# A fused attention and feed-forward kernel: a reordered beginning, and attention in fewer, wider steps

## The chip, the cores and the metric

The kernel runs on one core of a Trainium2 chip. The metric is the device time of one execution in microseconds, the median of several runs; less is better. One run was taken with the hardware profiler.

## The reference

```python
def _attn_ref(q, k, v, p):                      # q, k, v: (8, 8, 576, 64); p: (8, 8, 32, 64)
    scale = 1.0 / np.sqrt(q.shape[-1])
    def sm_attn(qq, kk, vv):
        s = scale * np.matmul(qq, kk.transpose(0, 1, 3, 2))
        s = s - np.max(s, axis=-1, keepdims=True)
        a = np.exp(s)
        a = a / (np.sum(a, axis=-1, keepdims=True) + 1e-09)
        return np.matmul(a, vv)
    p_packed = sm_attn(p, k, v)
    return sm_attn(q, p_packed, p_packed)

def _moe_ref(x, w_in, w_out):                   # x: (4608, 512); w_in: (512, 2048); w_out: (2048, 512)
    h = x @ w_in
    sp = np.where(h > 20.0, h, np.log1p(np.exp(np.minimum(h, 20.0))))
    g = h * np.tanh(sp)
    return (g @ w_out).astype(np.float32)
```

Per batch and head, 32 packed queries attend to 576 keys, which gives 32 packed values. The 576 queries then attend to those 32. The outputs of the 8 heads side by side are the 512 columns of x, which go through two matrices with a Mish between them. The inputs q, k, v, p are float32. The two weight matrices arrive as float64 and are converted on the core.

## The kernel before

The work goes batch by batch, 8 batches of 576 tokens. The second attention is never multiplied out: since x = a2 · p_packed, the kernel multiplies the packed values with w_in once per batch and chunk of 512 columns (`packed_w`, PSUM tile ps_w, split into wp_hi and wp_lo), and then the attention weights a2 (aT_hi and aT_lo) with that product. Each operand is split into a rounded high half and a low half, and three matmuls stand for one.

The main loop runs over 128 groups, one for each batch b and each of the 16 column blocks f of 128. Step t of the loop (`step`) does the up matmuls of group t (`up`, tile ps_h: two halves of six matmuls, each followed by ScalarE's Mish into g), the split of g into g_hi and g_lo (`halves`), and the down matmuls of group t − 2 (`down`: four accumulators acc of three matmuls each, weights wo). The order on TensorE in a step is: down 0, up 0, down 1, down 2, up 1, down 3. At the end of every fourth step, `packed_w` for the next chunk follows. Some steps also hold `down_rest` (tile ps_rest), the 64 tokens left over in two batches.

Between these pieces stand calls to two generators. `take(gen, ...)` advances the attention of the next batch by one step, up to three times in a step of the loop. `take(conv, ...)` advances the conversion of the weights: per weight, ScalarE writes two parts (`words`), VectorE joins them in four instructions (`join`, the last of which the profile names L390), and `done` writes them away or splits them (wo). w_in has 16 such weights, four for each chunk c (tile wi), and w_out has 16 (tile wo); the list `weights` says in which order.

Attention of one batch has these parts: turn the keys (transposes through PSUM, tile ps_kq, copied to kT by ScalarE and VectorE in turns), scores of the packed queries (ps_s) with their maximum and subtraction on VectorE, exponentials, the same turning for the queries (qT), row sums, transposes of the weights (tiles ps_a and a1T), the packed values (ps_pp, pp) and their transpose (ppT), the scores of all queries (`match`), and then `peak` and `weigh`, which make the second softmax on VectorE and ScalarE. From the third batch on, all its PSUM tiles come from the pool ps_a, which has two buffers of one bank each. packed_w and down_rest take theirs from the same pool.

TensorE's order is the order in which the code is written, throughout. In the beginning (attention of the first two batches, and the first 16 steps), the order on VectorE, ScalarE and SP's DMA queue is the written one too. From step 16 on, a scheduler with its own estimate of times sets the order on these three. Every engine works through its queue in order.

Of the kernel before, what the change touches and what calls it, by code (L numbers as in the profile page):

```python
# [35 lines left out]
def body(  # L36
# [101 lines left out]
    class Batch:  # L138
# [48 lines left out]

        def score(self, g, pool):

            kT = att.tile([P, NI, 4, R], F32, name="kT", tag="T", bufs=2)  # L190
            yield from transposed(pool, self.k_t[g], g, kT)
            s_ps = scores(pool, self.pT[:, g, :], kT)
            mx = stat.tile([P, 2], F32, name="mx")
            for u in range(2):
                nc.vector.reduce_max(out=mx[:, u:u + 1], in_=s_ps[u], axis=AX.X)
            top = stat.tile([P, 1], F32, name="top")
            nc.vector.tensor_tensor(out=top, in0=mx[:, 0:1], in1=mx[:, 1:2], op=ALU.max)
            for u in range(2):
                nc.vector.tensor_scalar(
                    out=self.a1[:, g, u].rearrange("a i r -> a (i r)"), in0=s_ps[u],  # L200
                    scalar1=top, scalar2=None, op0=ALU.subtract,
                )
            yield
# [42 lines left out]
        def turn_weights(self, g, pool):  # L246
            self.a1T[g] = att.tile([R, 2, NI, P], F32, name="a1T")
            for u in range(2):
                ps = psum(pool, [R, NI, P], "ps_a1")
                for i in range(NI):  # L250
                    nc.tensor.transpose(out=ps[:, i, :], in_=self.a1[:, g, u, i, :], identity=ident)  # L251
                evacuate(self.a1T[g][:, u], ps, ("ACT", "DVE")[u])
                yield

        def values(self, g, pool):
# [16 lines left out]
            yield  # L272

        def turn_values(self, g, pool):
            ps = psum(pool, [P, P], "ps_ppT")
            nc.tensor.transpose(out=ps, in_=self.pp[g].rearrange("a u d -> a (u d)"), identity=ident)
            nc.vector.tensor_copy(out=self.ppT[:, g, :], in_=ps)
            yield
# [5 lines left out]
        def match(self, g, pool):  # L284
# [7 lines left out]
            yield  # L292
# [12 lines left out]
        def weigh(self, gs):  # L305
# [9 lines left out]
            for g in range(gs.start, gs.stop):  # L315
                at = att.tile([P, S], F32, name="at", bufs=1)
                nc.vector.transpose(out=at, in_=self.a2[:, g].rearrange("a g n -> a (g n)"))
                nc.scalar.copy(out=self.aT_hi[:, g, :], in_=at)
                nc.vector.tensor_tensor(
                    out=self.aT_lo[:, g, :], in0=at, in1=self.aT_hi[:, g, :].bitcast(F32), op=ALU.subtract  # L320
                )

        def attention(self):
# [249 lines left out]
    weights = [Weight(0, m) for m in range(4)] + [WeightOut(0)] + [Weight(1, m) for m in range(4)]  # L573
    weights += [WeightOut(i) for i in range(1, 8)] + [Weight(2, m) for m in range(4)] + [WeightOut(8)]
# [22 lines left out]
    def step(t, n_att, n_conv, cast):  # L597
# [37 lines left out]
        if t % 4 == 2 and n < len(chunks):  # L635
# [12 lines left out]
    with tc.manual_schedule(engines={mybir.EngineType.PE}):  # L648
# [4 lines left out]
        with tc.manual_schedule(engines={mybir.EngineType.DVE, mybir.EngineType.Activation, mybir.EngineType.SP}):  # L653
# [26 lines left out]
            together(first.turn_weights(0, ps_acc))  # L680
# [6 lines left out]
            together(first.values(0, ps_a))  # L687
            together(first.turn_weights(1, ps_acc))
            w[2].words()
            w[2].join()  # L690
            together(first.values(1, ps_a))
            for g in range(2):
                together(first.turn_values(g, ps_a))
            w[3].words()
            for g in range(2):
                together(first.match(g, ps_acc))
# [10 lines left out]
            first.weigh(slice(0, 1))  # L707
# [15 lines left out]
            together(second.turn_weights(0, ps_acc))  # L723
            step(0, (0, 0, 0), 0, nc.scalar.copy)
            together(second.turn(1, ps_acc))
            second.sums_now(1, sums[1])
            w[4].words()
            w[4].join()
            together(second.values(0, ps_a))
            together(second.turn_weights(1, ps_acc))  # L730
            w[5].words()
            w[4].done()
            conv = conversion(5)
            together(second.values(1, ps_a))
            step(1, (0, 0, 0), 2, nc.scalar.copy)
            for g in range(2):
                together(second.turn_values(g, ps_a))
            for g in range(2):
                together(second.match(g, ps_acc))
            for g in range(2):  # L740
                second.peak(slice(g, g + 1))
            take(conv, 2)
            second.weigh(slice(0, 1))
            take(conv, 2)
            second.weigh(slice(1, 2))
            take(conv, 2)
            for t in range(2, START):
                step(t, (0, 0, 0), 3 if t < 8 or t == 11 else 1 if t == 10 else 2, nc.scalar.copy)
        for t in range(START, len(order) + LAG):
            if t in (16, 26):  # L750
                batches[t // 10 + 1].load()
            step(t, (1, 1, 1), 2, nc.vector.tensor_copy)
# [26 lines left out]
```

## Time and profile before

| | us |
|---|---|
| median of 3 runs (811.91 to 814.41) | 812.47 |
| the profiled execution | 809.08 |
| its span | 807.3 |
| TensorE busy in the span (95%) | 765.5 |
| VectorE busy (55%) | 441.9 |
| ScalarE busy (40%) | 323.2 |

PE is TensorE's matmuls and PEld its weight loads. DVE is VectorE, ACT is ScalarE, SP issues the DMAs. L and a number is a line of the kernel before. In a row of the timeline the start and the duration come first; a bracket at its end tells how long the engine stood idle before it, and what released it.

### The profile page before, as it was taken

The numbers are of one execution on the slowest core, as the hardware profiler recorded it, in microseconds if no ns is written. First come the engines' busy times: TensorE is split into PE (matmuls) and PEld (weight loads), VectorE is DVE, ScalarE is ACT, GpSimd is POOL, SyncE is SP. The second block draws the span as 40 slices with busy tenths as digits, with TensorE's granted clock in tenths as the row PEclk, the third lists the DMA queues.
The fourth block names the chain that finished last, engine by engine and source line by source line (L and its number), as shares of the span: only waits on it lengthen the run. The fifth ranks groups of instructions, "written<-read, shape, count | busy, mean of one in ns | idle before, by whom it ended". The sixth has DMA issues, their size and how long they took to land.

```text
span 807.3 us, 13715 instructions
## 1 busy us (share of the span) xinstructions
PE 765.5 (95%) x5584; PEld 608.5 (75%) x5584; DVE 441.9 (55%) x846; ACT 323.2 (40%) x752; POOL 0.7 (0%) x6
## 2 busy tenths in 40 slices
PE   7565799999999999999999999999999999999997
PEld 6344477887878787878788787888788787878886
DVE  4867887695457537354563546445473445532332
ACT  4353667563433424234342443334242343332221
POOL 0000000000000000000000000000000000000000
PEclk9667699999999999999999999999999999999999
DMA  9993205532522541242311532144311411131002
GB/s 251 302 293 113 104 27 157 161 127 79 172 90 79 158 141 59 76 138 92 111 53 59 176 96 76 56 154 125 112 53 53 137 40 54 53 105 53 1 1 65
DMA packets 42814, 85.82 MB, mean 106 GB/s; under 512 B 8448, under 2 KB 26880, under 8 KB 42752
## 3 DMA queue, kind: packets, MB, share of 16 engines
q1 hardware_dynamic: 42752, 84.95, 34.5%
q8 instruction: 44, 0.72, 0.4%
q14 instruction: 18, 0.15, 0.1%
HBM read 71.30 MB, written 13.63 MB: 105 GB/s over the span
## 4 chain that ended last, share of the span: by engine, by line
PE 88%; DVE 9%; ACT 2%; issue 1%; DMA 0%; SPq 0%; DVEq 0%; ACTq 0%
PE ps_h L479 25%; PE acc L496 15%; PE acc L498 14%; PE acc L497 14%; PE ps_w L428 4%; PE ps_kq L120 4%; PE ps_s L129 3%; PE ps_rest L496 2%; PE ps_rest L498 2%; PE ps_rest L497 2%; PE ps_pp L260 1%; PE ps_a L251 1%; DVE wi L387 1%; DVE wo L387 1%; DVE wo L390 1%
## 5 line engine op out<-in xcount | busy, mean ns | idle before, releaser
L496 PE MATMUL acc<-wo,g_hi 128*128 128x512 f32 x512 | 214.4, 419 | 1.9 <-ACT wo L411 1.1
L482 ACT ACTIVATE g<-ps_h 128x288 f32<-128x288 f32 (+1 forms) x256 | 98.2, 385 | 279.7 <-PE ps_h L479 229.2
L498 PE MATMUL acc<-wo,g_lo 128*128 128x512 f32 x512 | 202.6, 396 | 1.9 <-DVE g_lo L492 1.9
L497 PE MATMUL acc<-wo,g_hi 128*128 128x512 f32 x512 | 202.5, 395 | 0.0
L479 PE MATMUL ps_h<-aT_hi,wp_hi 128*128 128x288 f32 x512 | 157.6, 308 | 0.0
L491 DVE CAST g_hi<-g 128x512 fp32r<-128x512 f32 x112 | 47.8, 426 | 196.6 <-ACT g L482 196.6
L479 PE MATMUL ps_h<-aT_hi,wp_lo 128*128 128x288 f32 x512 | 152.8, 298 | 0.0
L479 PE MATMUL ps_h<-aT_lo,wp_hi 128*128 128x288 f32 x512 | 152.6, 298 | 0.0
L496 PEld LDWEIGHTS acc<-wo,g_hi 128*128 128x128 f32 x512 | 96.7, 189 | 45.1 <-issue 23.9
L498 PEld LDWEIGHTS acc<-wo,g_lo 128*128 128x128 f32 x512 | 96.8, 189 | 25.4 <-DVE g_lo L492 3.1
L479 PEld LDWEIGHTS ps_h<-aT_hi,wp_hi 128*128 128x128 f32 x512 | 97.6, 191 | 14.8 <-issue 5.6
L479 PEld LDWEIGHTS ps_h<-aT_lo,wp_hi 128*128 128x128 f32 x512 | 97.8, 191 | 8.8
L497 PEld LDWEIGHTS acc<-wo,g_hi 128*128 128x128 f32 x512 | 97.2, 190 | 8.6 <-DVE wo L412 0.4
L492 DVE TENSOR_TENSOR g_lo<-g,g_hi 128x512 fp32r<-128x512 f32 x128 | 88.2, 689 | 18.0 <-ACT g_hi L491 12.4
L479 PEld LDWEIGHTS ps_h<-aT_hi,wp_lo 128*128 128x128 f32 x512 | 97.7, 191 | 0.2 <-DVE wp_lo L440 0.2
L428 PE MATMUL ps_w<-wi,ppT 64*32 64x512 f32 x512 | 40.0, 628 | 13.7 <-DVE wi L390 10.1
L440 DVE TENSOR_TENSOR wp_lo<-ps_w,wp_hi 128x512 fp32r<-128x512 f32 x64 | 41.2, 682 | 19.1 <-ACT wp_hi L439 19.1
L439 ACT CAST wp_hi<-ps_w 128x512 fp32r<-128x512 f32 x64 | 34.4, 591 | 30.4 <-PE ps_w L428 30.4
L120 PEld LDWEIGHTS ps_kq<-ident,k_t 96*128 96x128 f32 x192 | 23.3, 162 | 6.8 <-issue 4.4
L484 ACT ACTIVATE g_rest<-ps_h 128x64 f32<-128x64 f32 x128 | 28.1, 219 | 0.0
L428 PEld LDWEIGHTS ps_w<-wi,ppT 64*32 64x32 f32 x512 | 6.4, 106 | 28.2 <-DVE wi L390 12.7
L120 PEld LDWEIGHTS ps_kq<-ident,q_t 96*128 96x128 f32 x192 | 21.9, 152 | 6.9 <-issue 3.0
(91 smaller groups left out, 753.4 us busy)
## 6 DMA issues: line engine op xcount, KB each, us to landing
wi<-w_in_f SPq DMA_DIRECT2D x48, 512.0 KB, 4.5
k_t<-in_k_dram SPq DMA_DIRECT2D x32, 288.0 KB, 3.6
q_t<-in_q_dram SPq DMA_DIRECT2D x32, 288.0 KB, 4.0
v_t<-in_v_dram SPq DMA_DIRECT2D x32, 288.0 KB, 3.9
w_st<-in_moe_w_in_dram SPq DMA_DIRECT2D x16, 512.0 KB, 6.4
w_st<-in_moe_w_out_dram SPq DMA_DIRECT2D x16, 512.0 KB, 4.4
out_dram<-o SPq DMA_DIRECT2D x24, 192.0 KB, 2.5
w_in_f<-wi SPq DMA_DIRECT2D x8, 512.0 KB, 4.8
```

The source lines that it names most:

```text
L120: nc.tensor.transpose(out=ps[:, h, :], in_=of_slot(src, g, h)[:, i, :], identity=ident[:R, :R])
L428: nc.tensor.matmul(out=ps[g][h * NP:(h + 1) * NP, :], lhsT=ppTb[row:row + D, g, h * NP:(h + 1) * NP], rhs=wis[c, g][row:row + D, h // 2, : ...
L439: nc.scalar.copy(out=hi, in_=ps[g])
L440: nc.vector.tensor_tensor(out=lo, in0=ps[g], in1=hi.bitcast(F32), op=ALU.subtract)
L479: nc.tensor.matmul(out=ps, lhsT=w[:, fs], rhs=a[:, g, cs], start=(n == 0), stop=(n == 5))
L482: nc.scalar.activation(out=self.act[:, hf * HALF:hf * HALF + m], in_=ps[:, :m], func=AF.Mish)
L484: nc.scalar.activation(out=self.g_rest[self.b % 2, self.f // 4][:, self.f % 4, :], in_=ps[:, m:], func=AF.Mish)
L491: cast(out=hi, in_=self.act)
L492: nc.vector.tensor_tensor(out=lo, in0=self.act, in1=hi.bitcast(F32), op=ALU.subtract)
L496: nc.tensor.matmul(out=acc, lhsT=hi[:, cs], rhs=wh, start=start, stop=False)
L497: nc.tensor.matmul(out=acc, lhsT=hi[:, cs], rhs=wl, start=False, stop=False)
L498: nc.tensor.matmul(out=acc, lhsT=lo[:, cs], rhs=wh, start=False, stop=stop)
```

## The change

It has two parts. In the beginning, the exponentials of the second batch's first scores go ahead of the first batch's weigh, and the second scores go ahead of packed_w. `weigh` is cut into `weigh`, `back` (transpose and high half) and `low` (low half). The second w_out weight is converted ahead of the second chunk of w_in. The conversions start with w4 as a generator, and steps 2 and 3 of the loop are put between peak and the two weighs. The second packed_w moves from the end of step 2 to the end of step 3.

From the third batch on, `attention` pauses less often. `turned` transposes two PSUM tiles for each call, one of them copied out by ScalarE and one by VectorE. The two tiles of the a1 transposes, the packed values of both halves and the two transposes ppT each go in one call. That is 17 calls in the place of 26 pauses and a last call, and a step of the loop from step 16 on calls it at most twice, not at most three times.

```diff
+        def turned(self, src, name):
+            n = 0
+            for g in range(2):
+                dst = att.tile([P, NI, 4, R], F32, name=name, tag="T", bufs=2)
+                (self.kTs if name == "kT" else self.qT)[g] = dst
+                for i in range(NI):
+                    ps = psum(ps_a, [P, 4, R], "ps_kq")
+                    for h in range(4):
+                        nc.tensor.transpose(
+                            out=ps[:, h, :], in_=of_slot(src[g], g, h)[:, i, :], identity=ident[:R, :R]
+                        )
+                    evacuate(dst[:, i, :, :], ps, ("ACT", "DVE")[n % 2])
+                    n += 1
+                    if n % 2 == 0:
+                        yield
...
         def attention(self):
             self.start(ps_a)
             yield
-            for g in range(2):
-                yield from self.score(g, ps_a)
+            self.kTs = {}
+            yield from self.turned(self.k_t, "kT")
+            for g in range(2):
+                self.score(g, ps_a)
+                yield
             self.exps(slice(0, 2))
-            for g in range(2):
-                yield from self.turn(g, ps_a)
+            yield from self.turned(self.q_t, "qT")
             self.sums()
             for g in range(2):
-                yield from self.turn_weights(g, ps_a)
-                yield from self.values(g, ps_a)
-            for g in range(2):
-                yield from self.turn_values(g, ps_a)
-            for g in range(2):
-                yield from self.match(g, ps_a)
+                self.turn_weights(g, ps_a)
+                yield
+            for g in range(2):
+                self.values(g, ps_a)
+            yield
+            for g in range(2):
+                self.turn_values(g, ps_a)
+            yield
+            for g in range(2):
+                self.match(g, ps_a)
+                yield
             self.peak(slice(0, 2))
             yield
             self.weigh(slice(0, 2))
+            for g in range(2):
+                self.back(g)
+                self.low(g)
...
-    weights = [Weight(0, m) for m in range(4)] + [WeightOut(0)] + [Weight(1, m) for m in range(4)]
-    weights += [WeightOut(i) for i in range(1, 8)] + [Weight(2, m) for m in range(4)] + [WeightOut(8)]
+    weights = [Weight(0, m) for m in range(4)] + [WeightOut(0), WeightOut(1)]
+    weights += [Weight(1, m) for m in range(4)] + [WeightOut(i) for i in range(2, 8)]
+    weights += [Weight(2, m) for m in range(4)] + [WeightOut(8)]
...
-        if t % 4 == 2 and n < len(chunks):
+        if t % 4 == (2 if t > 3 else 3) and n < len(chunks):
...
             second.score_now(0)
-            first.weigh(slice(0, 1))
             sums = [second.exps_now(0)]
             second.turn_keys(1)
...
+            first.weigh(slice(0, 1))
+            first.back(0)
+            second.score_now(1)
+            first.low(0)
+            sums.append(second.exps_now(1))
+            first.weigh(slice(1, 2))
+            first.back(1)
             wps = {(0, 0): packed_w(0, 0)}
-            second.score_now(1)
-            first.weigh(slice(1, 2))
-            sums.append(second.exps_now(1))
+            w[4].words()
+            first.low(1)
...
-            conv = iter(())
+            conv = conversion(4)
...
             take(conv, 2)
+            step(2, (0, 0, 0), 2, nc.scalar.copy)
             second.weigh(slice(0, 1))
-            take(conv, 2)
+            second.back(0)
+            take(conv, 1)
+            second.low(0)
+            take(conv, 1)
+            step(3, (0, 0, 0), 2, nc.scalar.copy)
             second.weigh(slice(1, 2))
-            take(conv, 2)
-            for t in range(2, START):
-                step(t, (0, 0, 0), 3 if t < 8 or t == 11 else 1 if t == 10 else 2, nc.scalar.copy)
+            second.back(1)
+            take(conv, 1)
+            second.low(1)
+            take(conv, 1)
+            for t in range(4, START):
+                step(t, (0, 0, 0), {4: 3, 5: 2, 6: 1, 7: 3}.get(t, 2), nc.scalar.copy)
...
-            step(t, (1, 1, 1), 2, nc.vector.tensor_copy)
+            step(t, (1, 1, 0), 2, nc.vector.tensor_copy)
```

The built programs show how the instructions stand. ScalarE's queue in the beginning, from the exponentials of the second batch's peak (tile a) on, before; wi and wround are the two parts of a conversion, aT_hi is the cast that belongs to a weigh, and g is the Mish of step 2:

```order
L303 ACT_TABLE_LOAD
L303 ACTIVATE a_798<-a_798 128x576 x2
L378 ACTIVATE wi<-w_st 128x512
L379 ACTIVATE wround<-w_st 128x512
L318 CAST aT_hi<-at 128x576
L378 ACTIVATE wi<-w_st 128x512
L379 ACTIVATE wround<-w_st 128x512
L318 CAST aT_hi<-at 128x576
L378 ACTIVATE wo_865<-w_st 128x512
L379 ACTIVATE wround<-w_st 128x512
L482 ACT_TABLE_LOAD
L482 ACTIVATE g<-ps_h 128x288
```

The same place now:

```order
L313 ACT_TABLE_LOAD
L313 ACTIVATE a_816<-a_816 128x576 x2
L402 ACTIVATE wi<-w_st 128x512
L403 ACTIVATE wround<-w_st 128x512
L506 ACT_TABLE_LOAD
L506 ACTIVATE g<-ps_h 128x288
L402 ACTIVATE wi<-w_st 128x512
L403 ACTIVATE wround<-w_st 128x512
L506 ACTIVATE g<-ps_h 128x224
L508 ACTIVATE g_rest_636<-ps_h 128x64
L515 CAST g_hi<-g 128x512
L330 CAST aT_hi<-at 128x576
```

The whole of step 2's Mish and its g_hi moved ahead of both casts aT_hi, of which the first closes the piece.

ScalarE's queue in a later batch, around its packed_w (wp_hi) and the exponentials of the next batch's first scores (L238; tile a), before:

```order
L482 ACTIVATE g<-ps_h 128x224
L484 ACTIVATE g_rest_3659<-ps_h 128x64
L439 CAST wp_hi<-ps_w_3848 128x512
L439 CAST wp_hi<-ps_w_3849 128x512
L482 ACTIVATE g<-ps_h 128x288
L238 ACT_TABLE_LOAD
L238 ACTIVATE a_3675<-a_3675 128x1152
L112 COPY qT<-ps_kq 128x384
L482 ACT_TABLE_LOAD
```

The same place now (the exponentials are L252):

```order
L506 ACTIVATE g<-ps_h 128x224
L508 ACTIVATE g_rest_3659<-ps_h 128x64
L252 ACT_TABLE_LOAD
L252 ACTIVATE a_3675<-a_3675 128x1152
L463 CAST wp_hi<-ps_w_3865 128x512
L463 CAST wp_hi<-ps_w_3866 128x512
L506 ACT_TABLE_LOAD
L506 ACTIVATE g<-ps_h 128x288
L112 COPY qT<-ps_kq 128x384 x2
```

The table load and the exponentials moved from behind packed_w's two casts to ahead of them.

VectorE's queue at that place, from the packed product's low halves (wp_lo) to the row sums of the exponentials (rs, L242), before:

```order
L440 TENSOR_TENSOR wp_lo<-ps_w_3848,wp_hi 128x512
L440 TENSOR_TENSOR wp_lo<-ps_w_3849,wp_hi 128x512
L195 TENSOR_REDUCE mx<-ps_s_3882 128x1
L195 TENSOR_REDUCE mx<-ps_s_3883 128x1
L197 TENSOR_TENSOR top<-mx 128x1
L199 TENSOR_SCALAR a_3675<-ps_s_3882,top 128x288
L199 TENSOR_SCALAR a_3675<-ps_s_3883,top 128x288
L242 TENSOR_REDUCE rs<-a_3675 128x2
```

The same place now, from the subtraction of the second scores on (the row sums are L256):

```order
L214 TENSOR_SCALAR a_3675<-ps_s_3832,top 128x288
L214 TENSOR_SCALAR a_3675<-ps_s_3833,top 128x288
L515 CAST g_hi<-g 128x512
L516 TENSOR_TENSOR g_lo<-g,g_hi 128x512
L256 TENSOR_REDUCE rs<-a_3675 128x2
L464 TENSOR_TENSOR wp_lo<-ps_w_3865,wp_hi 128x512
L257 TENSOR_SCALAR rs<-rs 128x2
L464 TENSOR_TENSOR wp_lo<-ps_w_3866,wp_hi 128x512
```

The second scores and the row sums moved ahead of the two wp_lo. The order is this one in all six batches that the later part treats.

More of the change, by code (lines that the diff above doesn't have):

```diff
@@ L186, in start @@
                 nc.vector.tensor_copy(out=pairs[0][:, :, t], in_=pairs[1][:, :, 1 - t])
+        def turned(self, src, name):
[13 more added lines that the diff above has]
+                        yield
         def score(self, g, pool):
-            kT = att.tile([P, NI, 4, R], F32, name="kT", tag="T", bufs=2)
-            yield from transposed(pool, self.k_t[g], g, kT)
-            s_ps = scores(pool, self.pT[:, g, :], kT)
+            s_ps = scores(pool, self.pT[:, g, :], self.kTs[g])
             mx = stat.tile([P, 2], F32, name="mx")
@@ L202, in score @@
                 )
-            yield
         def turn_keys(self, g):
@@ L271, in values @@
             )
-            yield
         def turn_values(self, g, pool):
@@ L277, in turn_values @@
             nc.vector.tensor_copy(out=self.ppT[:, g, :], in_=ps)
-            yield
         def turn(self, g, pool):
@@ L291, in match @@
                 nc.vector.transpose(out=a2f[:, u * HALF:(u + 1) * HALF], in_=s2[u])
-            yield
         def peak(self, gs):
@@ L314, in weigh, with back, low @@
             )
[L315 to L321, printed above, removed]
+        def back(self, g):
+            self.at = att.tile([P, S], F32, name="at", bufs=1)
+            nc.vector.transpose(out=self.at, in_=self.a2[:, g].rearrange("a g n -> a (g n)"))
+            nc.scalar.copy(out=self.aT_hi[:, g, :], in_=self.at)
+        def low(self, g):
+            nc.vector.tensor_tensor(
+                out=self.aT_lo[:, g, :], in0=self.at, in1=self.aT_hi[:, g, :].bitcast(F32), op=ALU.subtract
+            )
         def attention(self):
@@ L679, in body @@
             first.sums_now(0, sums[0])
-            together(first.turn_weights(0, ps_acc))
+            first.turn_weights(0, ps_acc)
             together(first.turn(1, ps_acc))
@@ L686, in body @@
             w[4].fetch()
-            together(first.values(0, ps_a))
-            together(first.turn_weights(1, ps_acc))
+            first.values(0, ps_a)
+            first.turn_weights(1, ps_acc)
             w[2].words()
             w[2].join()
-            together(first.values(1, ps_a))
+            first.values(1, ps_a)
             for g in range(2):
-                together(first.turn_values(g, ps_a))
+                first.turn_values(g, ps_a)
             w[3].words()
             for g in range(2):
-                together(first.match(g, ps_acc))
+                first.match(g, ps_acc)
             for g in range(2):
@@ L713, in body @@
                 w[n].fetch()
+            first.weigh(slice(0, 1))
[5 more added lines that the diff above has]
+            first.back(1)
             wps = {(0, 0): packed_w(0, 0)}
-            second.score_now(1)
-            first.weigh(slice(1, 2))
-            sums.append(second.exps_now(1))
+            w[4].words()
+            first.low(1)
             groups = []
             g_rests = [{} for _ in range(B // 2)]
-            conv = iter(())
+            conv = conversion(4)
             together(second.turn(0, ps_acc))
             second.sums_now(0, sums[0])
-            together(second.turn_weights(0, ps_acc))
-            step(0, (0, 0, 0), 0, nc.scalar.copy)
+            second.turn_weights(0, ps_acc)
+            take(conv, 1)
+            step(0, (0, 0, 0), 2, nc.scalar.copy)
             together(second.turn(1, ps_acc))
             second.sums_now(1, sums[1])
[L727 to L734, printed above, removed]
+            second.values(0, ps_a)
+            second.turn_weights(1, ps_acc)
+            take(conv, 2)
+            second.values(1, ps_a)
             step(1, (0, 0, 0), 2, nc.scalar.copy)
             for g in range(2):
-                together(second.turn_values(g, ps_a))
+                second.turn_values(g, ps_a)
             for g in range(2):
-                together(second.match(g, ps_acc))
+                second.match(g, ps_acc)
             for g in range(2):
```

2 lines of the change are left out of this document (1 added, 1 removed).

## The prediction

> **What bounds the kernel now.** I read the page first, then the stretches, the waits of TensorE (PE), and at last the rows of the stretches that the change touches.
>
> ```profile
> span 807.3 us, 13715 instructions
> PE 765.5 (95%) x5584; PEld 608.5 (75%) x5584; DVE 441.9 (55%) x846; ACT 323.2 (40%) x752; POOL 0.7 (0%) x6
> PEclk9667699999999999999999999999999999999999
> GB/s 251 302 293 113 104 27 157 161 127 79 172 90 79 158 141 59 76 138 92 111 53 59 176 96 76 56 154 125 112 53 53 137 40 54 53 105 53 1 1 65
> ```
>
> TensorE is busy 95% of the span; what it lacks, and the low granted clock, lie in the first fifth. The stretches say so more sharply (columns: length, then busy time of PE, PEld, DVE, ACT, POOL, then the clock):
>
> ```profile
> 0.00:160.00 160.00, 122.80 (x915) 92.06 (x916) 117.05 (x237) 85.63 (x187) 0.70 (x6) 0.84 0.60 177
> 160.00:800.00 640.00, 639.90 (x4660) 514.46 (x4659) 323.43 (x608) 237.51 (x566) 0.00 (x0) 1.00 0.28 88
> ```
>
> TensorE idles 37.2 us before 160 us and 0.1 us in the 640 after it. So the two halves of the change meet different ground. The beginning has something to win. In the rest, a step of attention wins only what its own matmuls cost beside the others, and any wait that it adds goes straight into the time.
>
> The largest pause of the beginning is at the second packed_w (tile ps_w, L428), whose weights (wi) are not converted yet:
>
> ```profile
> 51.07 0.59 PE L479 MATMUL ps_h<-aT_hi,wp_hi 128*128 128x288 f32 x1
> 74.21 1.04 PE L428 MATMUL ps_w<-wi,ppT 64*32 64x512 f32 x2
> 80.76 1.93 PE L428 MATMUL ps_w<-wi,ppT 64*32 64x512 f32 x8 [5.51 <-DVE wi L390]
> 87.29 1.93 PE L428 MATMUL ps_w<-wi,ppT 64*32 64x512 f32 x6 [4.60 <-DVE wi L390]
> 90.29 0.79 PE L496 MATMUL acc<-wo,g_hi 128*128 128x512 f32 x1 [1.08 <-ACT wo L411]
> 118.77 0.50 PE L498 MATMUL acc<-wo,g_lo 128*128 128x512 f32 x1 [1.25 <-DVE g_lo L492]
> ```
>
> 51.07 is the first up matmul of step 0, 90.29 the first down matmul of step 3, 118.77 the third of step 8. The idle time in brackets sums to 11.2 us, and the half clock that follows costs some 3 more.
>
> **The beginning, part by part.** No work is removed; conversions, weigh and steps change places. The prices (start and duration):
>
> ```profile
> 35.00 0.15 DVE L218 TENSOR_SCALAR top<-top 128x1 f32<-128x1 f32 x1
> 37.96 0.67 ACT L318 CAST aT_hi<-at 128x576 fp32r<-128x576 f32 x1 [5.74 <-DVE at L317]
> 80.62 0.74 DVE L309 TENSOR_REDUCE sm<-a 128x18 f32<-128x576 f32 x1
> 83.52 0.67 ACT L318 CAST aT_hi<-at 128x576 fp32r<-128x576 f32 x1 [4.73 <-DVE at L317]
> 84.90 0.42 DVE L383 TENSOR_SCALAR wi<-wi 128x512 f32<-128x512 f32 x1
> 87.16 0.42 DVE L383 TENSOR_SCALAR wo<-wo 128x512 f32<-128x512 f32 x1
> ```
>
> A conversion's join takes VectorE 2.26 us (84.90 to 87.16); a weigh 2.9 (80.62 to 83.52), then it waits for ScalarE's cast. ScalarE stands 5.74 us before that cast at 37.96, and the exponentials behind it could have started at 35.15, when top is written. Walking the new order with these and the neighbouring durations (an estimate by hand):
>
> 1. Exponentials ahead of weigh: the second batch's scores follow at 37.1; two weighs, the maxima, the two aT_lo then end on VectorE at 46.1, with packed_w hidden among them. Step 0's first up matmul comes at 46.9, not 51.07: 4.2 us ahead. The q transposes and first conversions move behind this, and the match ends about 3.6 ahead.
> 2. Steps 2 and 3 run before the second packed_w; they need wo0 and wo1, converted by 56.3. At 75.7 packed_w finds its last wi joined (75.15): the 11.2 us wait vanishes there. But step 4 needs wo2 (the third w_out weight) and the packed halves. VectorE has after the peak, which ends near 68.3, four joins (9.0), two g_lo and two wo low halves (2.7), a weigh with its aT_lo (3.7), two wp_lo (1.3) and short waits for ScalarE: 88.2. So TensorE waits from 76.8 to 83.4 and from 85.0 to 88.2, 9.8 us. The pause is not removed; it comes one step later in the work. One step is 4.4 to 7 us.
> 3. The second weigh now stands behind this. ScalarE's cast for it is ahead of two Mish and two conversions in its queue, so it holds them until 91.0; step 4's g_lo is done only at 102.4, which holds step 6 to 101.7. From there TensorE finds its inputs, and the 1.25 us wait at 118.77 has no counterpart: step 8's third down matmul at 112.6, 6.2 us ahead.
>
> SP's queue gets one w_out load ahead of the four w_in loads. Some 12 MB are issued up to the first of these; at the 251, 302 and 293 GB/s of the first three 20 us slices they have landed by 44, and its words are read near 53, so I cost that at nothing; without this cover it would cost up to 6 us. The conversions as a whole end one step later; the weights in question are first used two steps on: nothing. Term: **−6.2 us**. Ends: 0, where VectorE's conversions alone set step 8, to −14.2, where the whole pause with its cold clock goes and nothing comes for it. I stay near the walk.
>
> **The later batches.** The ten blocks of transposes or small matmuls fewer per batch (12 to 6 for k and q, 4 to 2 for a1, 2 to 1 for pp and for ppT) save switching on TensorE:
>
> ```profile
> 455.25 0.39 PE L498 MATMUL acc<-wo,g_lo 128*128 128x512 f32 x1
> 455.48 0.49 PE L120 MATMUL ps_kq<-ident,k_t 96*128 96x96 f32 x4
> 455.76 0.38 PE L479 MATMUL ps_h<-aT_hi,wp_hi 128*128 128x288 f32 x1
> 455.97 0.30 PE L479 MATMUL ps_h<-aT_lo,wp_hi 128*128 128x288 f32 x1
> 456.11 0.29 PE L479 MATMUL ps_h<-aT_hi,wp_lo 128*128 128x288 f32 x1
> ```
>
> Four transposes take 0.28; the first up matmul after them takes 0.21 instead of 0.14. A merged block saves 0.03 to 0.1: 0.5 us per batch, six batches, **−3 us** (ends 0 and −6).
>
> Against that stands one place. The pool ps_a has two banks, and each step now takes both. (That a group calls attention twice instead of three times costs nothing: it ends at f = 8, and is needed at f = 14.) At f = 2 of a batch the scores of both halves and packed_w follow each other, and at f = 3 the first q transposes. In the new order ScalarE runs the table load and the exponentials ahead of the wp_hi casts, and VectorE the row sums (L242) ahead of wp_lo, which frees the banks. The prices, on TensorE, VectorE, ScalarE:
>
> ```profile
> 446.50 0.72 PE L129 MATMUL ps_s<-kT,pT 64*32 64x288 f32 x16
> 447.14 0.41 PE L479 MATMUL ps_h<-aT_hi,wp_hi 128*128 128x288 f32 x1
> 457.43 1.09 PE L428 MATMUL ps_w<-wi,ppT 64*32 64x512 f32 x16
> 460.13 1.14 PE L129 MATMUL ps_s<-kT,pT 64*32 64x288 f32 x16
> ```
> ```profile
> 447.25 0.82 DVE L195 TENSOR_REDUCE mx<-ps_s 128x1 f32<-128x288 f32 x2 [0.65 <-PE ps_s L129]
> 448.31 0.94 DVE L199 TENSOR_SCALAR a<-ps_s,top 128x288 f32<-128x288 f32 x2
> 459.23 1.29 DVE L440 TENSOR_TENSOR wp_lo<-ps_w,wp_hi 128x512 fp32r<-128x512 f32 x2 [0.85 <-ACT wp_hi L439]
> 464.19 1.35 DVE L242 TENSOR_REDUCE rs<-a 128x2 f32<-128x1152 f32 x1 [1.23 <-ACT a L238]
> ```
> ```profile
> 458.61 1.07 ACT L439 CAST wp_hi<-ps_w 128x512 fp32r<-128x512 f32 x2 [1.30 <-PE ps_w L428]
> 460.71 1.28 ACT L238 ACT_TABLE_LOAD   x1
> 462.99 1.17 ACT L238 ACTIVATE a<-a 128x1152 f32<-128x1152 f32 x1 [1.00 <-DVE a L199]
> 464.54 1.28 ACT L482 ACT_TABLE_LOAD   x1
> 465.84 0.36 ACT L482 ACTIVATE g<-ps_h 128x224 f32<-128x224 f32 x1
> ```
>
> Count from the start of the first scores at f = 2. They take TensorE 0.64 (446.50 to 447.14); VectorE lets their banks go at 2.3 and 2.75 (446.50 to the end of L199). Six down matmuls at 0.23 (455.25 to 455.48) and the change of shape bring the second scores to 2.24: waits of 0.1 and 0.15. Their banks come back at 4.7 and 5.2; packed_w would start at 4.85: 0.35 more. It ends at 6.2; down and up of f = 3 bring TensorE to the q transposes at 7.75. ScalarE meanwhile: last Mish out at 4.75, table load to 6.0, exponentials to 7.2, first cast to 7.7. VectorE: row sums 7.25 to 8.55, first wp_lo to 9.2, second to 9.95. The transposes wait from 7.75 to 9.3, and between banks 0.45 more: 2.0. Together 2.6 a batch. Before, a wait of 0.42 (1.14 against 0.72) stood at f = 3; the same now stands at f = 7, where the second match follows packed_w. Some 0.2 behind other single transposes goes. Net 2.4, six times: **+14.4 us**. Ends: 0, where the exponentials end before packed_w, and 21, where the whole chain from 4.75 to 9.95, less the 1.7 that TensorE works, is waited for.
>
> Sum: −6.2 − 3 + 14.4 = +5.2. Against the profiled execution's own 809.08 that is 814.3; the runs' median stands 3.39 above it, so I forecast 817.5.
>
> Here a page of the Trainium skill speaks still harder against the change. ScalarE: Activation LUTs, section What ACT_TABLE_LOAD costs, has 1283 ns for the load and a drain of 1380 ns with each switch. By that the exponentials, and the wait, would end 1.38 us later, six times 8.3 us, near 826. The trace shows no such drain: load at 464.54, next Mish at 465.84, 1.30 later. I go by the row.
>
> **The rivals.** The bound for telling a change is 0.3%, 2.4 us: under 810.0, 810.0 to 814.9, over.
>
> *The half clock.* A wait of 2 us may halve the clock for the window after it:
>
> ```profile
> 57.90:61.30 3.40, 1.27 (x51) 1.10 (x44) 3.01 (x7) 1.45 (x3) 0.00 (x0) 1.00 0.96 223
> 61.30:64.70 3.40, 2.75 (x13) 2.33 (x11) 2.16 (x5) 1.45 (x5) 0.00 (x0) 0.50 0.60 180
> 115.90:119.40 3.50, 2.25 (x13) 1.57 (x11) 3.40 (x7) 2.52 (x7) 0.00 (x0) 1.00 0.26 54
> 119.40:122.80 3.40, 3.40 (x20) 2.92 (x19) 2.66 (x5) 1.69 (x4) 0.00 (x0) 1.00 0.40 119
> ```
>
> A window with 1.27 of 3.4 busy was followed by clock 0.50, one with 2.25 by 1.00. Mine has 1.5 to 1.9 if it holds the whole wait. Half a window each costs 1.7 us: six times 10, giving 828. TensorE: Matmul & The Clock Gate of the Trainium skill (section HAM oscillation — how this bites in real kernels) asks only that no idle gap pass about 3.4 us, and would rule this out; here 2.1 us of idle in one window sufficed. Chance 0.12.
>
> *The parts cancel (same).* If VectorE and ScalarE reach the bank-freeing casts about 1.2 us sooner, the wait is 1.2 a batch: 7 − 9 = −2, or 810 to 813. Chance 0.22.
>
> *The pause of the beginning truly goes (faster).* If ScalarE's casts do not hold the Mish of steps 4 and 5, the beginning gains up to 14.2: 14.4 − 17.2 gives 809.6. It decides from a gain of 13.8. For it speaks that the conversions are spread; against it VectorE's unbroken queue in point 2. Chance 0.12.
>
> *Two banks at once cost nothing (faster).* If the exponentials are over before packed_w ends, only −9.2 stays: 803.5. Against it stands the sequence 460.71 to 464.16, which must follow the last subtraction. Chance 0.08.
>
> **Numbers.** My forecast, 814.9 to 821, has 0.46. Below 808 lie most of the last rival, above 826 most of the clock's; the range 808 to 826 leaves out under 2 in 10. Slower 0.46 + 0.12 = 0.58, same 0.22, faster 0.20.
>
> **What would show it.** TensorE busy less than 640 of 640 us in the later stretch, with six waits of 1.3 to 2.2 us of ps_kq (q_t) on wp_lo, and the casts of wp_hi behind the exponentials: step right. No such waits: wrong, and the time falls to 804. For the beginning: packed_w without its two waits of 5.51 and 4.60, new waits on wo and wp_lo of 5 to 10 us ahead of step 4, step 8's third down matmul near 112.6. Were that at 105, the second rival of the faster side has it. A clock below 1.00 after 160 us would show the half clock.

## The result, and the profile after

The changed kernel takes 821.64 us in the median of four runs (821.47 to 824.77); the kernel before took 812.54 beside it (four runs, 811.91 to 814.41). The ratio is 1.0112, 95% interval 1.009 to 1.0135: slower by 9.1 us. The profiled execution is the slowest of the four, 824.77. The forecast was 817.5, range 808 to 826.

The page of the changed kernel, its size and the engines' busy time; below it two stretches (length, busy time of PE, PEld, DVE, ACT, POOL, then the granted clock, DMA share, GB/s):

```profile
span 823.0 us, 13706 instructions
PE 770.9 (94%) x5584; PEld 617.4 (75%) x5584; DVE 452.0 (55%) x858; ACT 317.0 (39%) x740; POOL 0.7 (0%) x6
```
```profile
0.00:160.00 160.00, 124.90 (x932) 95.76 (x933) 117.95 (x238) 86.37 (x191) 0.70 (x6) 0.82 0.60 174
160.00:800.00 640.00, 627.50 (x4564) 506.10 (x4563) 328.36 (x611) 226.90 (x539) 0.00 (x0) 0.99 0.29 89
```

Before, TensorE was busy 639.90 of the later 640 us, at clock 1.00. Now it is busy 627.50, at 0.99. The waits of TensorE from 160 us on (what waited, for what; sum, how often, longest) say what it now stands still for; before, this list was empty:

```profile
PE ps_kq L197 <- DVE wp_lo L464: 8.7, 6, 1.5
PE ps_h L503 <- ACT g L506: 1.5, 1, 1.5
PE ps_s L129 <- DVE a L214: 1.0, 6, 0.2
PE ps_kq L197 <- ACT kT L112: 0.6, 1, 0.6
```

Six waits of nearly 1.5 us: one per later batch, at f = 3, the q transposes on wp_lo, as forecast. One of them closely, in the timeline, on TensorE, ScalarE and VectorE:

```profile
463.91 1.11 PE L129 MATMUL ps_s<-kT,pT 64*32 64x288 f32 x16 [0.17 <-DVE a L214]
466.65 1.25 PE L452 MATMUL ps_w<-wi,ppT 64*32 64x512 f32 x16
471.05 1.22 PE L197 MATMUL ps_kq<-ident,q_t 96*128 96x96 f32 x8 [1.47 <-DVE wp_lo L464]
...
466.55 1.28 ACT L252 ACT_TABLE_LOAD   x1
467.84 1.17 ACT L252 ACTIVATE a<-a 128x1152 f32<-128x1152 f32 x1
468.92 1.05 ACT L463 CAST wp_hi<-ps_w 128x512 fp32r<-128x512 f32 x2
469.99 1.28 ACT L506 ACT_TABLE_LOAD   x1
...
469.04 1.35 DVE L256 TENSOR_REDUCE rs<-a 128x2 f32<-128x1152 f32 x1 [1.27 <-ACT a L252]
470.31 0.68 DVE L464 TENSOR_TENSOR wp_lo<-ps_w,wp_hi 128x512 fp32r<-128x512 f32 x1
470.98 0.68 DVE L464 TENSOR_TENSOR wp_lo<-ps_w,wp_hi 128x512 fp32r<-128x512 f32 x1
```

packed_w takes both banks at 466.65. ScalarE reaches the casts that release them only at 468.92, behind a table load and the exponentials; VectorE reaches the first wp_lo at 470.31, behind the row sums. TensorE gets the first bank back at 471.05, and the second only while it is in the block: that block takes 1.22 us, the next one like it, at 473.52, 0.82.

And the clock, the third figure from the end of such a row. In these traces it changes only on a grid of 3.41 us; the three pieces of half clock after 160 us begin at 204.02, 282.53 and 661.41 and last 3.41 each. Two of the six waits, each with the window of this grid that holds it and the window after it:

```profile
200.60:204.00 3.40, 1.87 (x13) 1.36 (x13) 2.69 (x5) 3.37 (x6) 0.00 (x0) 1.00 0.67 230
204.00:207.40 3.40, 3.40 (x12) 2.71 (x13) 0.56 (x1) 0.33 (x1) 0.00 (x0) 0.50 0.21 83
367.90:371.30 3.40, 1.95 (x14) 1.58 (x13) 2.25 (x4) 3.37 (x5) 0.00 (x0) 1.00 0.58 181
371.30:374.70 3.40, 3.28 (x26) 2.79 (x25) 1.30 (x4) 1.30 (x3) 0.00 (x0) 1.00 0.33 133
```

Both waits (1.42 and 1.45 us, ending at 203.26 and 371.06) lie whole in their window. The window with 1.87 of 3.40 busy was followed by half clock, the one with 1.95 was not. Of the other four, two lie in one window too, but for 0.05 us (busy 1.84 and 1.81), and were followed by half clock; two are shared by two windows, none of them under 67% busy, and were not. It happened behind three of the six.

The beginning, TensorE's rows (the second batch's first scores, step 0's first up matmul, the second packed_w, the waits at steps 4 and 6), then ScalarE's cast of the second weigh:

```profile
36.64 1.18 PE L129 MATMUL ps_s<-kT,pT 64*32 64x288 f32 x16 [2.95 <-ACT kT L112]
51.16 0.59 PE L503 MATMUL ps_h<-aT_hi,wp_hi 128*128 128x288 f32 x1
80.93 0.66 PE L452 MATMUL ps_w<-wi,ppT 64*32 64x512 f32 x8
87.97 0.79 PE L520 MATMUL acc<-wo,g_hi 128*128 128x512 f32 x1 [5.95 <-ACT wo L435]
92.15 0.61 PE L503 MATMUL ps_h<-aT_hi,wp_lo 128*128 128x288 f32 x1 [1.75 <-DVE wp_lo L464]
106.31 0.50 PE L520 MATMUL acc<-wo,g_hi 128*128 128x512 f32 x1 [2.00 <-ACT g_hi L515]
...
95.50 0.67 ACT L330 CAST aT_hi<-at 128x576 fp32r<-128x576 f32 x1 [5.70 <-DVE at L329]
```

packed_w no longer waits (5.51 and 4.60 before); step 4 waits instead, 5.95 for wo and 1.75 for wp_lo, and ScalarE stands 5.70 before the cast of the second weigh. In this execution step 0 begins no earlier than before (51.07), but the second batch's first scores began 4.4 us later; from them to step 0 it is 14.5 us, where before it was 18.8, from the row

```profile
32.28 1.22 PE L129 MATMUL ps_s<-kT,pT 64*32 64x288 f32 x16 [0.72 <-ACT kT L112]
```

Among the profiles of the new beginning that start lies between 33.1 and 36.6 us, so stretches are compared here, and totals by medians. In both profiles of the old beginning it lies earlier (32.28 and 33.01, the kernel before and one of the experiments); whether the new order of the weights delays it is not shown, and a stretch alone may flatter the new beginning.

### The profile page after: what moved, and what is told of

Read it like the earlier page. It is cut to its first block, busy times and chain, and to the rows that moved or that the text cites. A ratio compares the mean times of both kernels' runs of the same rounds, so it can differ in the third digit from the quotient of the medians.

```text
span 823.0 us, 13706 instructions
## 1 busy us (share of the span) xinstructions
PE 770.9 (94%) x5584; PEld 617.4 (75%) x5584; DVE 452.0 (55%) x858; ACT 317.0 (39%) x740; POOL 0.7 (0%) x6
## 4 chain that ended last, share of the span: by engine, by line
PE 80%; DVE 10%; ACT 5%; DMA 3%; issue 1%; SPq 1%; DVEq 0%; ACTq 0%
PE ps_h L503 23%; PE acc L520 14%; PE acc L522 13%; PE acc L521 13%; PE ps_s L129 3%; PE ps_kq L197 3%; PE ps_w L452 3%; PE ps_rest L520 2%; PE ps_rest L521 2%; PE ps_rest L522 2%; DMA w_st<-in_moe_w_out_dram 2%; PE ps_pp L273 1%; DMA w_st<-in_moe_w_in_dram 1%; PE ps_a L265 1%; DVE wp_lo L464 1%; DVE rs L256 1%
## 5 line engine op out<-in xcount | busy, mean ns | idle before, releaser
L503 PEld LDWEIGHTS ps_h<-aT_hi,wp_hi 128*128 128x128 f32 x512 | 98.4, 192 | 20.9 <-issue 5.7
L452 PE MATMUL ps_w<-wi,ppT 64*32 64x512 f32 x512 | 37.2, 615 | 2.0 <-ACT a L237 2.0
L197 PE MATMUL ps_kq<-ident,q_t 96*128 96x96 f32 x144 | 18.2, 268 | 9.5 <-DVE wp_lo L464 8.7
L197 PEld LDWEIGHTS ps_kq<-ident,q_t 96*128 96x128 f32 x144 | 15.3, 153 | 13.2 <-DVE wp_lo L464 11.9
L520 PE MATMUL ps_rest<-wo,r_hi 128*128 128x512 f32 x64 | 25.2, 393 | 0.0
```

The source lines that it names most:

```text
L197: nc.tensor.transpose(out=ps[:, h, :], in_=of_slot(src[g], g, h)[:, i, :], identity=ident[:R, :R])
L452: nc.tensor.matmul(out=ps[g][h * NP:(h + 1) * NP, :], lhsT=ppTb[row:row + D, g, h * NP:(h + 1) * NP], rhs=wis[c, g][row:row + D, h // 2, : ...
L503: nc.tensor.matmul(out=ps, lhsT=w[:, fs], rhs=a[:, g, cs], start=(n == 0), stop=(n == 5))
L520: nc.tensor.matmul(out=acc, lhsT=hi[:, cs], rhs=wh, start=start, stop=False)
```

## Experiments: the two halves apart

Each kernel was timed beside the kernel before, whose medians lay between 810.84 and 812.54 us. A difference between kernels of two groups of runs can be off by as much.

**The new beginning with the old attention.**

```
 for t in range(START, len(order) + LAG):
-    step(t, (1, 1, 0), 2, nc.vector.tensor_copy)
+    step(t, (1, 1, 1), 2, nc.vector.tensor_copy)   # attention() of before, 26 pauses
```

The lines that give attention() its old pauses back are left out here.

> The new beginning alone, with the attention of before in 26 steps from the third batch on. If the two halves add up, the beginning is worth what the lead at step 8 shows: 1.7 to 3.5 us in the profile of after, up to the 6.2 of the prediction. Then 806 to 810 us, TensorE busy 639.5 of 640 us after 160 us. Rival: the lead is only where the pauses stand in the first 120 us and is lost again by the conversions: 812.5 within 1.2.

Measured: 806.14 us, ratio to before 0.9924 (0.9906 to 0.9941): 6.3 us faster. After 160 us its one wait is 1.0 us. The beginning is worth what the prediction gave it, 6.2.

**The 17 steps with the old beginning.** The reverse: turned(), score() without its own transposes, the new attention() and (1, 1, 0) put into the kernel before.

> The 17 steps of two banks alone, with the beginning of before. Theory: six waits of 1.5 us of the q transposes on wp_lo as in after, and the half clock behind some of them; the beginning's gain of 2 to 6 us is missing, so 823.5 to 828 us. Rival: the beginning is worth nothing, 821.6 within 1.2.

Measured: 826.99 us, ratio 1.0191 (1.0174 to 1.0209): 14.6 us slower. The list of waits after 160 us reads like that of the changed kernel:

```profile
PE ps_kq L197 <- DVE wp_lo L461: 8.7, 6, 1.5
```

−6.3 and +14.6 make +8.3; both together measured +9.1. The halves add, within the spread of the medians.

## Experiments: what holds the banks

**The casts ahead of the exponentials.** In the changed kernel, with ScalarE's exponentials queued behind the second cast to wp_hi (VectorE's row sums, which need them, then follow wp_lo):

```
-            self.exps(slice(0, 2))
+            with tc.issue_after(last_cast["hi"].ins):
+                self.exps(slice(0, 2))
```

Left out are the lines that keep the last casts in `last_cast`, here and in the next experiment.

> After, with the exponentials (and so the row sums behind them) queued behind packed_w's casts to wp_hi. Theory of the prediction: the order in the two queues is what holds the banks; the six waits of 1.5 us and the half clock behind them go, 806 to 810 us. Rival: the 3.7 us that ScalarE is shut by two table loads and the exponentials must fall somewhere; now they stand ahead of the evacuation of the first q transposes, and the second pair waits 1.2 to 1.9 us for kT/qT's bank instead: 818 to 823 us.

Measured: 825.87 us, ratio 1.0181 (1.0154 to 1.0207): the rival in kind, and slower than its 818 to 823, some 4 us above the changed kernel. The wait on wp_lo is gone; another has taken its place, longer. The waits, then TensorE's and ScalarE's rows:

```profile
PE ps_kq L197 <- ACT qT L112: 10.6, 6, 1.8
```
```profile
470.78 0.88 PE L197 MATMUL ps_kq<-ident,q_t 96*128 96x96 f32 x8 [1.77 <-ACT qT L112]
...
466.17 1.28 ACT L252 ACT_TABLE_LOAD   x1
467.47 1.17 ACT L252 ACTIVATE a<-a 128x1152 f32<-128x1152 f32 x1
468.65 1.28 ACT L509 ACT_TABLE_LOAD   x1
470.25 0.47 ACT L112 COPY qT<-ps_kq 128x384 f32<-128x384 f32 x1
```

From 466.17 to 469.94, when a Mish follows, ScalarE is shut by two table loads and the exponentials. Whatever bank it has to empty in that time is held, and the next block that takes two banks waits for it. Behind three of these six waits, too, stands a window of half clock.

**The row sums behind wp_lo,** ScalarE's order as in the changed kernel:

```
-            self.sums()
+            with tc.issue_after(last_cast["lo"].ins):
+                self.sums()
```

> After, with VectorE's row sums queued behind packed_w's wp_lo; ScalarE's order as in after. If both queues hold the banks, the share of VectorE is 0.8 us of the wait: first wp_lo 0.5 after the first wp_hi cast, so 0.6 to 0.8 us are left of 1.5, and no window falls under the 55% busy below which the next one had half clock: batches of 90.8 to 91.1, 811 to 815 us. Rival: ScalarE alone sets it: batches of 91.7 and more, 819 us or more. Other rival, VectorE alone: the wait is gone, under 809 us.

Measured: 812.46 us, ratio 1.0008 (0.9989 to 1.0026): 9.2 us off the changed kernel with one order changed on VectorE.

```profile
PE ps_kq L197 <- DVE wp_lo L467: 4.0, 6, 0.7
```

Each wait falls from 1.5 to 0.7, and no window after 160 us has half clock. VectorE now stands idle before the first wp_lo, though the row sums could run:

```profile
461.39 1.29 DVE L467 TENSOR_TENSOR wp_lo<-ps_w,wp_hi 128x512 fp32r<-128x512 f32 x2 [1.74 <-ACT wp_hi L466]
```

So both queues hold the banks, each about half; and without the half that VectorE holds no window came near the busy share that half clock followed (the windows with these waits are 79% busy and more).

**Attention one group later.** `f == 0` becomes `f == 1` where the generator is made (and `t == 20` becomes 21), so that packed_w stands between k transposes and scores.

> After, with each batch's attention begun one group later, so that packed_w stands between the k transposes and the scores, not between the scores and the q transposes. Theory: it is the place, not the two banks; from the first of the second scores the q transposes come 3.7 us later and the banks are free at 2.8; the second pair waits at most 0.4 us for ScalarE: 806 to 810 us. Rival: two banks in one step cost wherever they stand: waits of 1 us or more somewhere in each batch, 816 us or more.

Measured: 815.03 us, ratio 1.0039 (1.0024 to 1.0054). Between the two theories: 6.6 us off the changed kernel, but the wait is 1.3, not 0.4.

```profile
469.67 0.88 PE L197 MATMUL ps_kq<-ident,q_t 96*128 96x96 f32 x8 [1.30 <-ACT qT L112]
465.07 1.28 ACT L252 ACT_TABLE_LOAD   x1
469.15 0.47 ACT L112 COPY qT<-ps_kq 128x384 f32<-128x384 f32 x1
```

I had let the table load begin while VectorE still subtracted; it begins behind the last Mish and a cast, 1.2 us later, so the same shut stretch of ScalarE meets the second pair of q transposes. At 1.3 us no window was followed by half clock.

**A group's pause behind the exponentials.** The changed kernel with two empty pauses:

```
             self.exps(slice(0, 2))
+            yield
+            yield
             yield from self.turned(self.q_t, "qT")
```

> After, with two empty pauses behind the exponentials, so that the first q transposes come one whole group (4.9 us) later than the casts of wp_hi. Theory: nothing is wrong with two banks as long as ScalarE's table loads and exponentials (3.7 us) have passed before the next transposes: no ps_kq wait over 0.3, batches of 89.5 to 90.2 us where after has 91.7 (or 93.3 with a half clock) and the new beginning alone 89.8; 804 to 808.5 us. Rival: the two banks cost again at another place (the values ahead of packed_w, the second match): batches of 91 or more, 812 us or more.

Measured: 806.15 us, ratio 0.9927 (0.9902 to 0.9951). The wait on wp_lo before the q transposes is gone, without any order in a queue being changed. Left are two small ones per batch:

```profile
PE ps_ppT L288 <- DVE wp_lo L466: 1.6, 6, 0.3
PE ps_s L129 <- DVE a L214: 1.0, 6, 0.2
```

**Pauses at every such place.** Two pauses at the start, one ahead of the scores, two behind the exponentials, one behind the row sums: the merged blocks are kept (and the third batch's generator is made at `t == 19`). That makes 23 steps, four more than with the group's pause alone; the text below miscounts them as six more and 26.

> e5 with six more empty pauses placed so that scores, packed_w and the steps behind it never follow one another within 1.4 us: 26 pauses as in before, but with the merged blocks of after. Theory: the two small waits left in e5 (0.17 of the second scores, 0.27 behind the packed_w of f = 6) go, and what is left of the merging is seen clean: even batches 89.2 to 89.5 us where e5 has 89.79, total 1.5 to 3 us below e5, 803 to 805.5 us. Rival: the merged blocks save nothing beyond what e5 shows: batches of 89.7 to 89.9, 806 within 1.5.

Measured: 800.33 us, ratio 0.9866 (0.984 to 0.9892), 5.8 below the kernel with one group's pause (5.0 by the ratios); better than either theory. No wait recurs batch by batch. One batch is the time from the first up matmul of its last group to the same matmul of the next batch; here those rows of the kernel before, the changed one and this one, two each:

```profile
434.18 0.29 PE L479 MATMUL ps_h<-aT_hi,wp_hi 128*128 128x288 f32 x1
524.05 0.29 PE L479 MATMUL ps_h<-aT_hi,wp_hi 128*128 128x288 f32 x1
```
```profile
442.42 0.29 PE L503 MATMUL ps_h<-aT_hi,wp_hi 128*128 128x288 f32 x1
534.13 0.29 PE L503 MATMUL ps_h<-aT_hi,wp_hi 128*128 128x288 f32 x1
```
```profile
428.51 0.29 PE L509 MATMUL ps_h<-aT_hi,wp_hi 128*128 128x288 f32 x1
516.99 0.29 PE L509 MATMUL ps_h<-aT_hi,wp_hi 128*128 128x288 f32 x1
```

89.87, 91.71 and 88.48 us. Every other batch holds most of the `down_rest` of a pair of batches and takes longer, 95.2, 97.3 and 94.0, with nearly the same differences. The reading over the other kernels, for a batch of the first kind (us):

| kernel | one batch | with half clock in it |
|---|---|---|
| before; new beginning alone | 89.8 | none |
| changed | 91.7 | 93.3 |
| casts first | none seen | 93.4 |
| one group later | 91.2 | none |
| row sums behind wp_lo | 90.85 | none |
| pause behind the exponentials | 89.79 | none |
| pauses at every place | 88.48 | none |

## Experiments: the beginning

The first two start from the new beginning alone (806.14).

**The second packed_w behind step 2 again:** `t % 4 == 2` for all steps.

> The new beginning alone (as e1), but the second packed_w stands behind step 2 again, as in before. Theory of the prediction (point 2): the move only carries the pause from packed_w to step 4; undone, packed_w waits some us for wi and step 4 that much less for wo: 806 to 809 us, the gain of 6.3 comes from the exponentials and conversions ahead of the weighs. Rival: the move is the gain: 811 us or more.

Measured: 807.46 us, ratio 0.9939 (0.9918 to 0.9961), which the spread does not tell from 806.14. The wait changes its name: packed_w waits 2.5 for wi, and wo 4.8 in two pieces.

**The weighs ahead of the exponentials again,** and the first packed_w ahead of the second scores:

```
             second.score_now(0)
+            first.weigh(slice(0, 1)); first.back(0); first.low(0)
             sums = [second.exps_now(0)]
...
-            first.weigh(slice(0, 1)); first.back(0)
+            wps = {(0, 0): packed_w(0, 0)}
             second.score_now(1)
-            first.low(0)
-            sums.append(second.exps_now(1))
-            first.weigh(slice(1, 2)); first.back(1)
-            wps = {(0, 0): packed_w(0, 0)}
-            w[4].words(); first.low(1)
+            first.weigh(slice(1, 2)); first.back(1); first.low(1)
+            sums.append(second.exps_now(1)); w[4].words()
```

> The new beginning alone (as e1), but the two weighs of the first batch stand ahead of the second batch's exponentials again, and the first packed_w ahead of the second scores. Theory (point 1): ScalarE stands 5.7 us before the cast of aT_hi and the second scores come 3 to 4 us later; step 8 and the end come 2 to 4 us later: 808 to 810.5 us. Rival: the lead at step 0 is eaten by the conversions that VectorE has to do in any case: 806 within 1.

Measured: 811.55 us, ratio 0.9985 (0.9966 to 1.0005): 5.4 of the 6.3 us are lost, more than the 2 to 4 I expected. From the second batch's first scores to step 0 it takes 18.8 us again, as before; in the new beginning alone, 14.3:

```profile
35.89 1.21 PE L129 MATMUL ps_s<-kT,pT 64*32 64x288 f32 x16 [3.39 <-ACT kT L112]
50.15 0.38 PE L511 MATMUL ps_h<-aT_hi,wp_hi 128*128 128x288 f32 x1
```
```profile
36.80 0.73 PE L129 MATMUL ps_s<-kT,pT 64*32 64x288 f32 x8 [3.52 <-ACT kT L112]
55.60 0.59 PE L511 MATMUL ps_h<-aT_hi,wp_hi 128*128 128x288 f32 x1
```

**The second batch's weighs two steps later.** From the kernel with a group's pause (806.15):

```
-            second.weigh(slice(0, 1)); second.back(0); take(conv, 1); second.low(0); take(conv, 1)
+            take(conv, 2)
             step(3, (0, 0, 0), 2, nc.scalar.copy)
-            second.weigh(slice(1, 2)); second.back(1); take(conv, 1); second.low(1); take(conv, 1)
+            take(conv, 2)
             for t in range(4, START):
                 step(t, ...)
+                if t in (4, 5):
+                    second.weigh(slice(t - 4, t - 3)); second.back(t - 4); second.low(t - 4)
```

> e5 with the second batch's two weighs behind steps 4 and 5, not ahead of steps 3 and 4. They are needed by step 8 alone. Theory (point 3 of the prediction seen from the other side): VectorE's 3.9 us of the first weigh stand in the queue ahead of wo2, for which TensorE waits 6.0 us at step 4; that wait falls to 1.5 to 2.5 us and the half clock behind it shrinks; step 8 begins 4 to 8 us earlier and the total is 798 to 803 us. Rival: VectorE's work up to step 8 is what bounds the beginning, in whatever order: the wait only moves to steps 5 to 8, 805 to 807 us.

Measured: 803.11 us, ratio 0.9898 (0.9877 to 0.9919): 3.0 us less (2.4 by the ratios), the weak edge of the theory. Step 4's wait for wo falls from 5.95 to 1.69. But ScalarE now stands twice for 3.62 before a weigh's cast, with Mish behind it, for which TensorE waits 1.47 and 2.65; the second time:

```profile
104.45 0.67 ACT L330 CAST aT_hi<-at 128x576 fp32r<-128x576 f32 x1 [3.62 <-DVE at L329]
...
105.49 0.40 PE L505 MATMUL ps_h<-aT_hi,wp_hi 128*128 128x288 f32 x1 [2.65 <-ACT g L508]
```

**Pauses and later weighs together.**

> The pauses of e9 and the later weighs of e10 together. They lie in different stretches (behind and ahead of 160 us), so the gains add: 806.15 less 5.8 less 3.0 is 797.3, 795.5 to 799 us. Rival: the half clock or the conversions in the stretch from 120 to 200 us take the weighs' gain back: 799.5 us or more.

Measured: 797.63 us, ratio 0.9822 (0.9783 to 0.9862). They add, within a wide spread.

**The same, with ScalarE's cast one step behind each weigh.** `back` is cut into turn_back, VectorE's transpose, and cast_back, ScalarE's cast.

```
-                if t in (4, 5):
-                    second.weigh(slice(t - 4, t - 3)); second.back(t - 4); second.low(t - 4)
+                if t in (5, 6):
+                    second.cast_back(t - 5); second.low(t - 5)
+                if t in (4, 5):
+                    second.weigh(slice(t - 4, t - 3)); second.turn_back(t - 4)
```

> e11 with ScalarE's cast aT_hi of each weigh one step behind the weigh, so that ScalarE does not stand before it with the next Mish in its queue (it stood 3.62 us twice in e10, and TensorE waited 1.47 and 2.65 us for the Mish). Theory, as in point 1 of the prediction: a cast that waits holds the Mish behind it; both waits and the half clock behind the second go, 3 to 6 us below e11: 791.5 to 795 us. Rival: another input of the same steps (wo, g_lo) is late by as much: within 1 us of e11.

Measured: 796.5 us, ratio 0.9794 (0.9767 to 0.9822), the fastest kernel of the study, 2.1% below the kernel before and 3.1% below the changed one. The total is only 1.1 below the last, which its spread does not tell from nothing; it lies between the theory and its rival. In the profile the two waits for Mish are gone, and the stretch from step 2 to step 9 takes 45.2 us where it took 48.9; a wait of 1.2 for g_lo has come instead. That the medians show less than the stretch stays open.

## Why the prediction was right, and where its sizes were off

1. **The beginning, −6.2.** Measured −6.3. Point 1 held in its size: 4.2 us forecast from the exponentials ahead of the weighs, 4.3 to 4.5 measured between first scores and step 0 (18.8 to 14.5 and 14.3). It carries more of the gain than the walk gave it (5.4 of 6.3 by the medians, where the first packed_w moved as well). Point 2 held in kind: 9.8 us of new waits forecast at step 4, 5.95 + 1.75 found; moving packed_w alone could not be told from nothing (1.3 by the medians). Of point 3, ScalarE's stand before the second weigh's cast is there (5.70 at 95.50), and step 6 was to begin its down matmuls late, and does (2.00 at 106.31). The order of the w_out conversions was not undone by itself. The forecast of 112.6 for step 8 failed in absolute time (117.19); counted from the first scores the lead is 5.9 us, where 6.2 was forecast.

2. **The wait at f = 3.** Place, waiting tile, releaser and the two causes were right: 1.55 us for the first bank forecast, 1.47 found. The smaller waits of that place, between banks, are not in the list but in the lengths of the rows: 0.17 and 0.39 at the second scores (1.11 against 0.72), 0.16 in packed_w (1.25 against 1.09), 0.40 in the q transposes (1.22 against 0.82). With the 1.47 that is 2.6, the 2.6 of the count. The experiment with the casts first qualifies the cause: it is not the order of the casts but a ScalarE that is shut for 3.7 us while every step needs it to empty a bank.

3. **The terms of the later batches.** Per batch 2.4 of waits less 0.5 of saving, net 1.9, was forecast; 1.9 was measured without half clock (91.71 against 89.8). Both terms were too small. With the pauses at every place a batch takes 88.48, 1.3 less than before. About 0.4 of this is a wait of the kernel before: its second scores, behind packed_w, took 1.14 (460.13 in the prediction's rows), and here, away from packed_w, they take no longer than the first:

```profile
454.53 0.72 PE L129 MATMUL ps_s<-kT,pT 64*32 64x288 f32 x16
458.36 0.71 PE L129 MATMUL ps_s<-kT,pT 64*32 64x288 f32 x16
```

About 0.9 is left for the merged blocks, an estimate from one batch: 5.4 us for six, where the sum has 3. In the same way the waits that the change adds are 1.9 and 0.9, some 2.8 a batch, near 17 us for six, where the sum has 14.4. That the two errors cancel is luck. (The sum's 814.3 and 3.39 make 817.7; the forecast says 817.5.)

4. **The half clock** is what the sum left out. Without it, −6.3 and six times 1.9 on 812.5 give 817.6, the forecast; the measured 821.64 has some 4 us more. I made it a rival of "1.7 us, six times" at 0.12. In the profiles it came behind three waits of six in the changed kernel, two in the old beginning with the new attention and three with the casts first, at 1.6 us each (93.3 against 91.7). How often it came in the runs that were not profiled is not known; for the new attention alone 6 × 1.9 + 2 × 1.6 is 14.6, as its medians have it. So it is no all-or-nothing rival; each wait met it or not, and it belonged into the sum at about half its price.

5. **The other rivals.** "Two banks cost nothing" was wrong of this order and right of the idea: with the pauses they gain. "The pause of the beginning truly goes" would have needed weighs that do not stand ahead of wo2 and casts that do not hold Mish; moving both took the kernel with all pauses from 800.33 to 796.5 us (5.8 us by the ratios).

6. **The two rules of the Trainium skill.** ScalarE shows 1.29 us from the table load to the next activation (466.55 to 467.84), and 1.29 again at 469.99 (the Mish follows at 471.28). The drain of 1380 ns that ScalarE: Activation LUTs, section What ACT_TABLE_LOAD costs, adds to a load does not stand there; the trace decides, as the prediction had it. TensorE: Matmul & The Clock Gate, section HAM oscillation — how this bites in real kernels, would have kept the clock up, since no gap of the later stretch came near 3.4 us; here a wait of 1.5 us was enough for half clock three times in six.

## What to carry to other kernels

Before work is merged into steps that take all the banks of a pool, look for the longest stretch in which an engine that empties them is shut (here two table loads and an exponential, 3.7 us), and leave that much other work before the next step; empty pauses turned a loss of 9 us into a gain of 11 (6 of it the beginning's). In an in-order queue, look at what stands ahead of the instruction that another engine waits for: exponentials ahead of a weigh's cast that waited 5.7 us gave most of 5 us, and row sums behind the two subtractions that free the banks gave 9, though VectorE then stood idle. And price a recurring wait of TensorE with its clock, by whether it can fill nearly half of one 3.4 us window.

## What the runs showed of the hardware

In the later stretch of these profiles, eight windows of 3.41 us at full clock with TensorE busy 48 to 55% were each followed by a window at half clock; all the others, one of 55% (1.86 of 3.40, at 173.0 with pauses and later weighs together) and those of 56% and more, were followed by full clock. For that stretch the edge lies at 55%. It is no rule on the busy share alone, for in the beginning it did not hold: in the changed kernel a window with 1.77 of 3.40 busy was followed by full clock (below), and in the kernel with pauses at every place one with 2.11, at 20.9, by half.

```profile
101.60:105.00 3.40, 1.77 (x9) 1.29 (x9) 2.76 (x5) 2.01 (x5) 0.00 (x0) 1.00 0.01 2
105.00:108.40 3.40, 2.01 (x10) 1.54 (x11) 2.65 (x6) 2.93 (x7) 0.00 (x0) 1.00 0.00 0
```

All eight windows hold a wait of 1.4 to 1.8 us whole, or all but 0.06 us of it. Waits shared by two windows in larger parts were not followed by half clock. Nor is lying whole enough: the window of the changed kernel with 57% holds its wait whole too. Waits of 1.3 us were never followed by half clock in the later stretch. So one kernel's waits cost 1.5 or 3.1 us, according to how they and the other short gaps fall on the windows.
